# Where the key weights are loaded and the first tiles are normalised in a transformer block's forward and backward pass

## The chip, the cores and the metric

The kernel runs on one core of one Trainium2 chip. The metric is device time in microseconds, the median of several executions; lower is better. The engines are TensorE (PE; its weight loads are PEld), VectorE (DVE), ScalarE (ACT), GpSimd (POOL) and SyncE (SP), which only issues DMAs here. Each engine works through its own queue in program order.

## The reference

One block of a transformer with 2048 rows of width 640, and the gradients of all its inputs:

```python
h  = x + A_ref(layernorm(x), wqkv, wo)         # linear attention, 32 heads of 20
h2 = h + B_ref(layernorm(h), w1, w3, w2)       # silu(x @ w1) * (x @ w3) @ w2, F = 1728
# in A_ref:
q, k, v = split(x @ wqkv)
phi = lambda t: where(t > 0, t + 1, exp(t)) + 1e-6
pq, pk = phi(q), phi(k)
kv = einsum("bhsd,bhse->bhde", pk, v);  z = sum_s(pk)
o = (pq @ kv) / (pq . z + 1e-6);        return o @ wo
```

The outputs are h2 and the gradients of x, wqkv, wo, w1, w3 and w2 for a given `grad_out`, all bfloat16. `layernorm` takes the mean off a row and divides by the root of its variance plus 1e-5.

## The kernel before, in words

The 2048 rows are 16 tiles (ST) of 128 rows; the width of 640 is 5 chunks (DT) of 128, or two halves (HD) of 320. The order of all work is written out by hand: whatever is emitted first on an engine runs first there, and a DMA is issued in the order of the queue that issues it.

**The start (L115 to L195).** SP issues x tile 0, tile 1, the first column half of the key weights (`load_wq(2, 3)`), x tile 2, the second half (`load_wq(3, 4)`), x 3, x 4 and 5; then transposing loads of `w2T` and of the output's gradient (`g2T`), and the rest of x. ScalarE first runs one tiny Exp, which loads its table. TensorE runs 34 warm-up matmuls (L468).

**A tile's way through the first loop (L528 ff.).** For each tile t:
1. VectorE takes statistics (`stat`, L148 two `bn_stats`, L151 the aggregate, L154 variance plus epsilon), and POOL the power of -1/2 (L155, `ln_rs`).
2. `p1_norm` (L247) normalises x in place, on VectorE (L161), for tiles 10, 12 and 14 on ScalarE (L166, which needs a bias that POOL makes at L170). From tile 8 on it also issues a DMA transpose into `pqT` (L251).
3. Up to tile 7, `p1_tr` (L253) transposes the five chunks on TensorE into a PSUM tile `tr`, and ScalarE copies it to `pqT` (L260).
4. `p1_mm` (L274) multiplies the turned tile by the key weights, in two halves of five matmuls (L268), into a PSUM tile `big` of which there are two. The transposes of tile t+1 are emitted between the two halves (`between`).
5. `phi` (L290) has ScalarE read the sums twice, Exp (L295) into `mq` and Relu (L296) into `rq`, three buffers each; its two closing instructions on VectorE (L299, L300) are held back in a list `held` and emitted later.

Tile 0 is an exception (RAW = 1): its x is only centred, and the factor is given to ScalarE as the scale of its activations (L535); its keys use two PSUM tiles of their own, so that ScalarE can start on the first half. `p1_scale` (L262) multiplies x of tile 0 afterwards, on VectorE (L264).

The table `v_steps` says what VectorE does in step t of the loop, in this order: ("S", n) statistics of tile n, ("N", n) `p1_norm`, ("C", n) `p1_scale`, and R, which takes the oldest pair out of `held`. The letters A, B and L are `p1_norm` calls that come after `phi(t)`. Where t stands in `QT` = (6, 7, 9, 11), `q_tile` does the query product of tile 0, 1, 2, 3 in the same way as the keys, after the "A" step. In steps 3 to 6 `ghh_chunk` adds five matmuls of 512 columns (L395), which need `w2T` and `g2T`. From step 7 on `m_part` (L425) accumulates phi(k)ᵀ x over the tiles (needing the finished x of those tiles), and x is stored to DRAM (`xn_out`).

**After the loop** come more query tiles, the heads' denominators (`r_prod` on POOL, L367, `r_row` on VectorE, `r_T` DMA transposes), `load_w2T(4 * P, 8 * P)` (L624), and, when the last `m_part` is done, the reload of x tiles 0 to 5 (L641, for the residual). `f2_wT` (L701) then makes the product weights `Wp` and turns them by DMA transposes (L709); the first use of `Wp` is at L657.

**Later stages.** `q_parts` (L1205) makes the five blocks of QT, each turned by a DMA transpose on SP (L1226), while `load_xnT` (L1237) issues transposing loads on the same queue; the third of these stands before `part(20)` (L1315), which emits the rest of `q_parts`. The next product (L1388) reads all of QT. The last stage (L1556 ff.) makes the gradients of w1 and w3 in 35 jobs; the results of the first seven are stored in two pieces each.

Of the kernel before, what the change touches and what calls it, by code (L numbers as in the profile page):

```python
# [55 lines left out]
def kernel(  # L56
# [74 lines left out]
    class Stats:  # L131
# [13 lines left out]
        def part(self, src, t, j, mid=None):  # L145
            if j == 0:
                self.st[t] = cp.tile([P, 2, 6], F32, name="st6", bufs=4)
            V.bn_stats(out=self.st[t][:, j, :], in_=src[:, t, j * HD:(j + 1) * HD])  # L148
            if j == 0:
                return  # L150
            V.bn_aggr(out=self.mv[:, t, :], in_=self.st.pop(t)[:])  # L151
            if mid is not None:
                mid()
            V.tensor_scalar(out=self.ve[:, t:t + 1], in0=self.mv[:, t, 1:2], scalar1=EPS_LN, scalar2=None, op0=ALU.add)  # L154
            G.tensor_tensor(out=self.rs[:, t:t + 1], in0=self.ve[:, t:t + 1], in1=mhalf[:, 0:1], op=ALU.pow)  # L155
# [86 lines left out]
    RAW = 1  # L242
# [10 lines left out]
    def p1_tr(t, parts=((0, DT),)):  # L253
        xn = x_sb[:, t, :]
        for a, b in parts:
            tr = ps.tile([P, DT, P], BF16, name="tr", bufs=2)
            for c in range(a, b):
                T.transpose(tr[:, c, :], xn[:, c * P:(c + 1) * P], ident[:])

            A.copy(out=pqT[:, a:b, t * P:(t + 1) * P], in_=tr[:, a:b, :])  # L260
# [29 lines left out]
    def phi(acc, dst, t, parts=None):  # L290

        mq, rq = parts or phi_tiles()
        if parts is None:
            kw = dict(scale=ln1.rs[:, t:t + 1]) if t < RAW else {}
            A.activation(two(mq[:]), acc[:, :, 0:HD], AF.Exp, **kw)  # L295
            A.activation(two(rq[:]), acc[:, :, 0:HD], AF.Relu, **kw)  # L296

        def rest():
            V.tensor_scalar(out=mq[:], in0=mq[:], scalar1=1.0, scalar2=1e-6, op0=ALU.min, op1=ALU.add)  # L299
            V.tensor_tensor(out=dst, in0=mq[:], in1=rq[:], op=ALU.add)  # L300
        held.append(rest)
# [201 lines left out]
    def load_wo():  # L503
# [24 lines left out]
    for t in range(ST):  # L528
        first = None
        if t < RAW:  # L530
            first = phi_tiles()
            kh = [ps.tile([P, 512], F32, name="k0", tag="m", bufs=2) for _ in range(2)]

            def act(i, j):
                A.activation(first[i][:, j * HD:(j + 1) * HD], kh[j][:, 0:HD], (AF.Exp, AF.Relu)[i],  # L535
                             scale=ln1.rs[:, t:t + 1])

            def between():
                act(0, 0)
                p1_tr(t + 1)  # L540
                act(1, 0)
            k = p1_mm(t, D, between, kh)
            act(0, 1)
            act(1, 1)
        else:
# [78 lines left out]
    load_w2T(4 * P, 8 * P)  # L624
# [3 lines left out]
    m_part(4, range(5))  # L628
    q_tile(8)
# [11 lines left out]
    load_x(0, 6)  # L641
# [302 lines left out]
    def kv3():  # L944
# [5 lines left out]
        (f2_wT, 4), (phi_rest,), (q_late, 14), (r_T, 4), (r_head, 5), (r_prod, 7),  # L950
# [654 lines left out]
```

## Time and profile before

| what | us |
|---|---|
| median of 3 runs | 819.78 (819.46 to 819.9) |
| the profiled execution's own time | 820.36 |
| its span, first to last instruction | 818.6 |
| TensorE busy in the span | 811.6 |
| VectorE, ScalarE, GpSimd busy | 452.7, 324.8, 131.7 |
| first key matmul of tile 0 | 6.61 |
| key matmuls of tile 3 | 12.68 |

The tables below are read so: a timeline row has the start in us from the span's start, the duration in us, the engine, the line, the operation, what it writes <- reads, the shapes, the count, and in brackets the idle time before it and what ended that. A row with a count above 1 has several instructions merged, and its duration runs to the end of the last. Idle time of an engine that is not the bottleneck costs nothing.

### The profile page before, as it was taken

To read this page: it belongs to the slowest core of one execution; us is meant where nothing else is said; L and a number is where in the kernel's file an instruction comes from. 1 tells how busy PE (TensorE), PEld (TensorE's weight loads), DVE (VectorE), ACT (ScalarE), POOL (GpSimd) and SP (SyncE) were. 2 spreads that over 40 slices of the span, in tenths; PEclk is the share of its full clock that TensorE was granted. 3 is DMA by queue.
4 is the path that set the end of the run, shared out by engine and by line. 5 is a ranking of instruction groups with operands and counts; after the bars stand their busy time and mean duration, and the time that the engine had idled before them with its cause. 6 is when DMAs were issued, how large, how long until landed. Compare 5 with 4: busy or idle time off the path is not lost.

```text
span 818.6 us, 13711 instructions
## 1 busy us (share of the span) xinstructions
PE 811.6 (99%) x5261; PEld 501.6 (61%) x5292; DVE 452.7 (55%) x973; ACT 324.8 (40%) x609; POOL 131.7 (16%) x198
## 2 busy tenths in 40 slices
PE   9999999999999999999999999999999999999998
PEld 6777544555555555754577777777777777544444
DVE  7859997998898566300057777772781544200000
ACT  7856688665565666011112212222212334211111
POOL 2243333323222212100001111110220000000000
PEclk9999999999999999999999999999999999999999
DMA  9899899696485556999877877269994888979991
GB/s 262 207 242 277 206 276 302 207 244 174 128 209 158 169 168 168 239 254 243 233 178 181 218 194 193 58 111 181 269 217 93 179 193 153 249 175 235 221 239 37
DMA packets 335889, 162.46 MB, mean 198 GB/s; under 512 B 252560, under 2 KB 329072, under 8 KB 335824
## 3 DMA queue, kind: packets, MB, share of 16 engines
q1 hardware_dynamic: 291920, 120.68, 63.8%
q0 software_dynamic: 7328, 24.48, 8.9%
q10 hardware_dynamic: 36576, 16.42, 8.2%
q8 instruction: 41, 0.67, 0.3%
q14 instruction: 24, 0.20, 0.1%
HBM read 47.09 MB, written 53.43 MB: 123 GB/s over the span
## 4 chain that ended last, share of the span: by engine, by line
PE 96%; DMA 1%; ACT 1%; DVE 1%; issue 0%; SPq 0%; POOL 0%; DVEq 0%
PE mm L395 20%; PE job L1335 19%; PE ghn L1131 14%; PE gxn L1504 8%; PE gw L1086 7%; PE big L268 4%; PE o L913 4%; PE o L859 3%; PE gwo L1219 3%; PE macc L430 3%; PE gr L1188 3%; PE dkv L1441 3%; PE at L657 2%; DMA wqkv<-in_A_wqkv_dram 1%; PE dkv L1369 1%; DMA tri<-tri 1%
## 5 line engine op out<-in xcount | busy, mean ns | idle before, releaser
L1335 PE MATMUL job<-gb,hnN 128*128 128x496 bf16 (+3 forms) x576 | 116.8, 366 | 0.0
L1131 PEld LDWEIGHTS <-ggb 128*128 128x128 bf16 x864 | 84.5, 98 | 33.0
L395 PE MATMUL mm<-pqT,w 128*128 128x512 bf16 x396 | 93.2, 379 | 0.5
L1335 PEld LDWEIGHTS <-hnN 128*128 128x128 bf16 x576 | 55.8, 98 | 61.0
L395 PEld LDWEIGHTS <-w 128*128 128x128 bf16 x540 | 52.6, 98 | 62.9 <-issue 0.6
L1339 ACT CAST obs<-job 128x496 bf16<-128x496 f32 (+4 forms) x56 | 28.5, 510 | 123.6 <-PE job L1335 123.6
L1131 PE MATMUL ghn<-w13a,ggb 128*128 128x320 bf16 x448 | 63.5, 299 | 0.0
L1146 DVE SCALAR_TENSOR_TENSOR wb<-gs,hnb 128x640 f32<-128x640 bf16 x16 | 13.2, 825 | 88.1 <-ACT gs L1143 88.1
L1131 PE MATMUL ghn<-w13b,ggb 128*128 128x320 bf16 x416 | 61.4, 299 | 0.0
L395 PE MATMUL mm<-g2T,w2T 128*128 128x512 bf16 x228 | 58.8, 379 | 0.6
L1086 PE MATMUL gw<-hb,g 128*128 128x512 bf16 (+2 forms) x316 | 58.4, 345 | 0.2
L1086 PEld LDWEIGHTS <-g 128*128 128x128 bf16 x320 | 31.3, 98 | 27.0
L420 ACT CAST ghh<-mm 128x512 bf16<-128x512 f32 x48 | 28.2, 588 | 48.2 <-PE mm L395 41.4
L1196 POOL TENSOR_TENSOR sz<-Zb,g_h 128x640 f32<-128x640 bf16 x16 | 20.2, 1262 | 163.7 <-DVE g_h L1197 163.7
L796 ACT ACTIVATE sig<-mm 128x512 bf16<-128x512 f32 x56 | 33.7, 602 | 25.0 <-PE mm L395 21.6
L1143 ACT ACTIVATE gs<-ghn 128x640 bf16<-128x640 f32 x16 | 11.3, 705 | 76.0 <-PE ghn L1131 76.0
L395 PEld LDWEIGHTS <-w2T 128*128 128x128 bf16 x260 | 25.4, 98 | 23.4
L268 PEld LDWEIGHTS <-pqT 128*128 128x128 bf16 x320 | 30.7, 98 | 13.5 <-ACT pqT L260 0.9
L268 PE MATMUL big<-wqkv,pqT 128*128 128x320 bf16 x250 | 38.4, 299 | 0.2
L1335 PEld LDWEIGHTS <-g 128*128 128x128 bf16 x320 | 31.0, 98 | 11.5
L832 DVE TENSOR_TENSOR gate<-gate,sig 128x1024 bf16<-128x1024 bf16 x28 | 19.3, 689 | 33.9 <-ACT gate L807 31.1
L1091 ACT CAST gw2o<-gw 128x512 bf16<-128x512 f32 (+2 forms) x20 | 10.4, 519 | 66.6 <-PE gw L1086 25.3
(217 smaller groups left out, 1391.2 us busy)
## 6 DMA issues: line engine op xcount, KB each, us to landing
hh_d<-hhT SPq DMA_DIRECT2D x24, 256.0 KB, 2.8
gg_d<-gate POOLq DMA_DIRECT2D x24, 256.0 KB, 4.4
gg_d<-ghh POOLq DMA_DIRECT2D x24, 256.0 KB, 4.1
ggb<-gg_d SPq DMA_DIRECT2D x6, 896.0 KB, 5.3
ggb<-gg_d ACTq DMA_DIRECT2D x6, 832.0 KB, 5.7
ggb<-gg_d SPq DMA_DIRECT2D x2, 1728.0 KB, 13.9
pk_d<-pk_all SPq DMA_DIRECT2D x4, 640.0 KB, 5.4
g<-in_grad_out_dram SPq DMA_DIRECT2D x4, 640.0 KB, 5.7
```

Source lines behind the costliest of these rows:

```text
L268: T.matmul(acc, lhsT=pqT[:, c, t * P:(t + 1) * P], rhs=wqkv[:, c, n0:n0 + HD], start=(c == 0), stop=(c == DT - 1))
L395: T.matmul(acc[:], lhsT=w[:, c, fc * P:(fc + 1) * P], rhs=rhs[:, c, :], start=(c == 0), stop=(c == DT - 1))
L420: A.copy(out=ghh[n // 2][:, n % 2, :], in_=acc[:])
L430: T.matmul(macc[m][j][:, 0:n], lhsT=pk_all[:, t, m * P:(m + 1) * P], rhs=x_ext[:, t, j * HD:j * HD + n], start=(t == 0), stop=(t == ST - 1))
L796: A.activation(sig[:, i, :], gp[:], AF.Sigmoid)
L859: T.matmul(accs[i, j][:, 0:HD], lhsT=hhT[c][:, fc, i * P:(i + 1) * P], rhs=w2[:, fc, j * HD:(j + 1) * HD], start=(first and fc == 0), stop ...
L913: T.matmul(o2["ps"][:, 0:HD], lhsT=hhT[c][:, fc, i * P:(i + 1) * P], rhs=w2[:, fc, j * HD:(j + 1) * HD], start=(fc == 0), stop=(fc == FT - 1))
L1086: T.matmul(acc[:, 0:fw], lhsT=g2[:, t, m * P:(m + 1) * P], rhs=hb[b][:, t, 0:fw], start=(t == 0), stop=(t == ST - 1))
L1131: T.matmul(acc[:, j, 0:HD], lhsT=ggb[t // 2][:, k, lo:lo + P], rhs=rhs[:, j * HD:(j + 1) * HD], start=(k == 0), stop=(k == NG - 1))
L1335: T.matmul(acc[:, 0:n], lhsT=lhs[:, t, m * P:(m + 1) * P], rhs=rhs(t), start=(t == 0), stop=(t == ST - 1))
L1339: A.copy(out=ob, in_=acc[:, 0:n])
L1504: T.matmul(acc[:, j, 0:HD], lhsT=g, rhs=wqT[:, k, j * HD:(j + 1) * HD], start=(k == 0), stop=(k == 14))
```

## The change

- The key weights are loaded by ScalarE's queue in two pieces of rows (chunks 0 and 1, then chunks 2 to 4, all 640 columns), and x tiles 4 and 5 by that queue too; SP issues x tiles 1, 2 and 3 ahead of everything else.
- `first_mm` does tile 0's keys chunk by chunk, both halves in a `big` tile, with the transposes of tile 1 after the second chunk.
- RAW = 5: tiles 0 to 4 are only centred, and the factor goes to ScalarE's activations. `p1_scale` multiplies those tiles of x later, now on GpSimd.
- VectorE in place of ScalarE copies the turned tiles 2 and 3 out of PSUM; from t = 3 on, the transposes of tile t+1 come after both halves of tile t.
- `v_steps` is written anew for this, and four of eight further warm-up matmuls are left out.
- x tiles 0 to 3 are reloaded before the `w2T` load, which is moved behind `r_head(3)` and `m_part(4, range(5))` and split in two; tiles 4 and 5 are reloaded after `f2_wT(4)`.
- `load_xnT(2)` comes after `part(20)`; five instead of seven jobs store in two pieces.

```diff
-        def part(self, src, t, j, mid=None):
+        def part(self, src, t, j, mid=None, end=True):
...
-            if j == 0:
-                return
+            if j and end:
+                self.end(t, mid)
+
+        def end(self, t, mid=None):
             V.bn_aggr(out=self.mv[:, t, :], in_=self.st.pop(t)[:])
...
+    def load_wk(a, b):
+        A.dma_start(out=wqkv[:, a:b, D:2 * D], in_=wq_v[:, a:b, D:2 * D])
+
+    for t in (1, 2, 3):
+        load_x(t, t + 1)
     A.activation(sg[:], zero[:], AF.Exp)
-    load_wq(2, 3)
-    load_x(2, 3)
-    load_wq(3, 4)
-    load_x(3, 4)
-    load_x(4, 6)
+    load_wk(0, 2)
+    load_wk(2, DT)
+    load_x(4, 6, A.dma_start)
...
-    RAW = 1
+    RAW = 5
...
-            A.copy(out=pqT[:, a:b, t * P:(t + 1) * P], in_=tr[:, a:b, :])
+            copy(out=pqT[:, a:b, t * P:(t + 1) * P], in_=tr[:, a:b, :])
 
     def p1_scale(t):
         xn = x_sb[:, t, :]
-        V.tensor_scalar(out=xn, in0=xn, scalar1=ln1.rs[:, t:t + 1], scalar2=None, op0=ALU.mult)
+        G.tensor_scalar(out=xn, in0=xn, scalar1=ln1.rs[:, t:t + 1], scalar2=None, op0=ALU.mult)
...
+    def first_mm(between):
+        acc = p1_acc()
+        for c in range(DT):
+            for j in range(2):
+                T.matmul(acc[:, j, 0:HD], lhsT=pqT[:, c, 0:P], rhs=wqkv[:, c, D + j * HD:D + (j + 1) * HD],
+                         start=(c == 0), stop=(c == DT - 1))
+            if c == 1:
+                between()
+        return acc
...
-    warm_up(8, p1_acc()[:, 0])
-    stat(1)
-    p1_norm(1)
-    ln1.part(x_sb, 2, 0)
-    ln1.part(x_sb, 2, 1)
+    warm_up(4, p1_acc()[:, 0])
+    for t in (1, 2):
+        ln1.part(x_sb, t, 0)
+        ln1.part(x_sb, t, 1, lambda: center(t))
     ln1.part(x_sb, 3, 0)
-    p1_norm(2)
-    ln1.part(x_sb, 3, 1)
-    ln1.part(x_sb, 4, 0)
-    p1_norm(3)
-    ln1.part(x_sb, 4, 1)
+    ln1.part(x_sb, 3, 1, end=False)
...
-    v_steps = {1: (R, ("N", 4)), 2: (("S", 5), R, ("N", 5)), 3: (("S", 6), R, ("N", 6), ("C", 0)),
-               4: (("S", 7), R, ("N", 7), ("S", 8)), 5: (R, ("N", 8), ("S", 9)), 6: (R, ("N", 9), ("S", 10)),
-               7: (("S", 11), R, R, ("A", 10), ("L", 11)), 8: (("S", 12), R, R, ("S", 13)),
-               9: (("N", 13), R, ("S", 14), ("B", 12)), 10: (R, R, ("S", 15)), 11: (R, ("A", 14), ("L", 15))}
-    V_OPS = {"S": stat, "N": p1_norm, "C": p1_scale}
+    v_steps = {1: (("E", 3), ("P", 4, 0)), 2: (("P", 4, 1), ("E", 4), R), 3: (("S", 5), R, ("N", 5), ("C", 0)),
+               4: (("S", 6), R, ("N", 6), ("C", 1)), 5: (("S", 7), R, ("N", 7), ("S", 8), ("C", 2), ("C", 3)),
+               6: (R, ("N", 8), ("S", 9), ("C", 4)), 7: (R, R, ("N", 9), ("S", 10), ("S", 11), ("A", 10), ("L", 11)),
+               8: (("S", 12), R, R, ("S", 13)), 9: (("N", 13), R, ("S", 14), ("B", 12)), 10: (R, R, ("S", 15)),
+               11: (R, R, ("A", 14), ("L", 15))}
+    V_OPS = {"S": stat, "N": p1_norm, "C": p1_scale, "E": lambda t: ln1.end(t, lambda: center(t)),
+             "P": lambda t, j: ln1.part(x_sb, t, j, end=False)}
...
-            k = p1_mm(t, D, (lambda: p1_tr(t + 1)) if t + 1 < XT_DMA else None)
+        turn = (lambda: p1_tr(t + 1, copy=V.tensor_copy if t in (1, 2) else A.copy)) if t + 1 < XT_DMA else None
+        k = p1_mm(t, D, turn, int(t > 2)) if t else first_mm(turn)
...
-    load_w2T(4 * P, 8 * P)
     dmaG(out=m_v[:, 1:4, :], in_=mbs[:, 1:4, :])
     r_head(3)
     r_prod(5)
     m_part(4, range(5))
+    load_x(0, 4)
+    load_w2T(4 * P, 6 * P)
+    load_w2T(6 * P, 8 * P)
...
-    load_x(0, 6)
...
-        (f2_wT, 4), (phi_rest,), (q_late, 14), (r_T, 4), (r_head, 5), (r_prod, 7),
+        (f2_wT, 4), (load_x, 4, 6), (phi_rest,), (q_late, 14), (r_T, 4), (r_head, 5), (r_prod, 7),
...
+    part(20)
     load_xnT(2)
-    part(20)
...
-                halves = ((a, c), (c, b)) if i * DT + m < 7 else ((a, b),)
+                halves = ((a, c), (c, b)) if i * DT + m < 5 else ((a, b),)
```

More of the change, by code (lines that the diff above doesn't have):

```diff
@@ L184, in load_wq, with load_x @@
         dma(out=wqkv[:, :, a * HD:b * HD], in_=wq_v[:, :, a * HD:b * HD])
-    def load_x(a, b):
-        dma(out=x_sb[:, a:b, :], in_=xS[:, a:b, :])
-    load_x(1, 2)
-    A.activation(sg[:], zero[:], AF.Exp)
-    load_wq(2, 3)
-    load_x(2, 3)
-    load_wq(3, 4)
-    load_x(3, 4)
-    load_x(4, 6)
+    def load_x(a, b, q=dma):
+        q(out=x_sb[:, a:b, :], in_=xS[:, a:b, :])
+    def load_wk(a, b):
+        A.dma_start(out=wqkv[:, a:b, D:2 * D], in_=wq_v[:, a:b, D:2 * D])
+    for t in (1, 2, 3):
+        load_x(t, t + 1)
+    A.activation(sg[:], zero[:], AF.Exp)
+    load_wk(0, 2)
+    load_wk(2, DT)
+    load_x(4, 6, A.dma_start)
     mask = cp.tile([P, DT, M_MAX], BF16, name="mask")
@@ L251, in p1_norm, with p1_tr @@
             dmaT(out=pqT[:, :, t * P:(t + 1) * P], in_=xn)
-    def p1_tr(t, parts=((0, DT),)):
+    def p1_tr(t, parts=((0, DT),), copy=A.copy):
         xn = x_sb[:, t, :]
@@ L272, in p1_acc, with p1_mm @@
         return ps.tile([P, 2, 512], F32, name="big", bufs=2)
-    def p1_mm(t, n0, between=None, halves=None):
-        acc = p1_acc() if halves is None else None
+    def p1_mm(t, n0, between=None, at=0):
+        acc = p1_acc()
         for j in range(2):
-            p1_half(acc[:, j, 0:HD] if halves is None else halves[j][:, 0:HD], t, n0 + j * HD)
-            if j == 0 and between is not None:
+            p1_half(acc[:, j, 0:HD], t, n0 + j * HD)
+            if j == at and between is not None:
+                between()
+        return acc
+    def first_mm(between):
+        acc = p1_acc()
+        for c in range(DT):
[3 more added lines that the diff above has]
+            if c == 1:
                 between()
@@ L288, in phi_tiles, with phi @@
         return [p1.tile([P, D], BF16, name=n, bufs=3) for n in ("mq", "rq")]
[L290 to L296, printed above, removed]
+    def phi(acc, dst, t):
+        mq, rq = phi_tiles()
+        kw = dict(scale=ln1.rs[:, t:t + 1]) if t < RAW else {}
+        A.activation(two(mq[:]), acc[:, :, 0:HD], AF.Exp, **kw)
+        A.activation(two(rq[:]), acc[:, :, 0:HD], AF.Relu, **kw)
         def rest():
@@ L528 @@
     for t in range(ST):
[L529 to L545, printed above, removed]
-            k = p1_mm(t, D, (lambda: p1_tr(t + 1)) if t + 1 < XT_DMA else None)
+        turn = (lambda: p1_tr(t + 1, copy=V.tensor_copy if t in (1, 2) else A.copy)) if t + 1 < XT_DMA else None
+        k = p1_mm(t, D, turn, int(t > 2)) if t else first_mm(turn)
         steps = v_steps.get(t, (R,) * len(held))
@@ L551 @@
             elif step[0] in V_OPS:
-                V_OPS[step[0]](step[1])
-        phi(k, pk_all[:, t, :], t, first)
+                V_OPS[step[0]](*step[1:])
+        phi(k, pk_all[:, t, :], t)
         for when in ("A", "B", "L"):
```

## The prediction

> **What bounds the kernel now.** I read the page's busy shares, then the chain that ended last, then the engines' busy time by stage, then the timeline of the first 40 us.
>
> ```profile
> PE 811.6 (99%) x5261; PEld 501.6 (61%) x5292; DVE 452.7 (55%) x973; ACT 324.8 (40%) x609; POOL 131.7 (16%) x198
> ...
> PE 96%; DMA 1%; ACT 1%; DVE 1%; issue 0%; SPq 0%; POOL 0%; DVEq 0%
> ```
>
> TensorE carries the chain and hardly ever waits: the most a better order can give is the few microseconds in which it does. But over the whole span VectorE at 55% hides a stage. Busy time by stage (us of PE, PEld, DVE, ACT, POOL):
>
> ```profile
> 6.20:14.00 7.80, 6.99 (x61) 4.46 (x59) 6.59 (x20) 6.38 (x12) 2.04 (x4) 1.00 1.12 256
> 14.00:25.00 11.00, 10.89 (x78) 7.00 (x78) 10.14 (x34) 10.16 (x17) 2.58 (x5) 1.00 0.96 311
> ```
>
> From 14 to 25 us VectorE works 10.1 of 11 us: in the tile loop it is nearly as full as TensorE. The timeline shows TensorE's waits at the start, and behind them ScalarE waiting for VectorE:
>
> ```profile
> 6.61 0.84 PE L268 MATMUL k<-wqkv,pqT 128*128 128x320 bf16 x5 [0.18 <-DMA wqkv<-in_A_wqkv_dram]
> ...
> 8.14 0.84 PE L268 MATMUL k<-wqkv,pqT 128*128 128x320 bf16 x5 [0.41 <-DMA wqkv<-in_A_wqkv_dram]
> ...
> 10.73 0.52 PEld L268 LDWEIGHTS <-pqT 128*128 128x128 bf16 x5 [0.44 <-ACT pqT L260]
> ...
> 12.68 0.52 PEld L268 LDWEIGHTS <-pqT 128*128 128x128 bf16 x5 [0.44 <-ACT pqT L260]
> ...
> 29.15 0.70 ACT L295 ACTIVATE mq<-big 128x640 bf16<-128x640 f32 x1 [0.20 <-DVE pk_all L300]
> ...
> 32.40 0.70 ACT L295 ACTIVATE mq<-big 128x640 bf16<-128x640 f32 x1 [0.76 <-DVE pk_all L300]
> ```
>
> Two waits are for key weights, two for ScalarE's copy of a turned tile. Two more follow later, 0.4 us at 85.6 (Wp's transposes) and 0.5 us at 566.5:
>
> ```profile
> 558.77 3.34 SPq L1242 DMA_TRANSPOSE xnT<-xn_d  x1
> ...
> 562.21 1.22 SPq L1226 DMA_TRANSPOSE tri<-tri  x1
> ...
> 566.50 0.78 PE L1388 MATMUL gkvT<-tri,woT 128*128 128x140 bf16 x10 [0.47 <-DMA tri<-tri]
> ```
>
> **Start.** Tile 0's own chain stays; its second ScalarE copy starts near 5.6, and other rows give 0.74 from such a copy's start to the next matmul (9.99 to 10.73): first matmul at 6.25, not 6.61. The weights: before, two column halves landed at 6.6 and 8.1 (issue 1.73 + 4.8, 2.77 + 5.3). Now ScalarE issues them after its first activation ends (2.30), three DMAs of about 0.5 each (SP rows 0.43 to 0.52), done by 3.8, before its first work at 4.50 (0.7 of cover; what exceeds it would delay tile 0). The first piece is only 320 KB. 560 KB (x tile 2 and the second half) took the 1.5 us between the halves, so x 2, x 3 and piece 1 (640 KB) need about 1.8 us from 3.1: 5 to 5.5. Piece 2 (480 KB), beside w2T's transposes, which SP now issues from about 2.7 and not 4.3: 6.3 to 8.1; I take 6.9, and 7.1 is when it is needed. Then, at 0.136 us a matmul and 0.056 a transpose: tile 1 starts at 8.0 (was 8.82). VectorE's copies of tiles 2 and 3 out of PSUM are not in the trace; L1422's copies take 0.28 at 256 columns and 0.35 at 384, so 0.49 at 640, at most ScalarE's 0.69; I take 0.49. The copy starts 0.49 after the transposes: tile 2 at 9.7 (10.73), tile 3 at 11.4 (12.68). **Gain 1.3.** The four warm matmuls left out (4 x 0.107) ran in waiting time. From tile 3 on the transposes come after both halves: ScalarE's copy then hides under ghh_chunk (5 matmuls, 1.08).
>
> **VectorE's account decides whether that gain lives.** From start-to-start times in the rows: a statistic S 1.23 (0.91 stats pair, 0.245, 0.075), a rest R 0.83 (0.42 + 0.41), a norm N 0.36, a centring 0.30. After the first copy (9.60): E3, half of 4, the wait for and copy of tile 3 (to 11.3), half of 4, E4, R: 13.2. Step 3 (S R N, 2.42) 15.6; step 4 18.05; step 5 (two S) 21.7; step 6 24.1; step 7 (R R N S S, 4.48) 28.6. N11 now has no R ahead of it to hide POOL's power (0.77 wait, as before at 35.06: 0.67), 29.7; S12 30.95; then at last the R of q_tile(0), 31.8. Before, that R ended at 29.9 (29.40 + 0.49). mq and rq are three deep, so phi(8) waits for it: 31.9 instead of 30.34, ends at 33.3; only then is the second "big" bank free for q_tile(2), which before started at 32.10 (30.74 + 1.36). The same happens once more, since q_tile(1)'s R now stands behind N13's wait: q_tile(3) at 39.5, before 37.81. **The gain is used up and 1.7 us lost**, with no cost yet for the scaling moved to GpSimd. Scaled activations (0.79 for 0.70) and the first wait behind N5 (0.26) are inside these sums.
>
> **The five scalings on GpSimd.** This operation isn't in the trace on POOL. Its neighbours: a product of 320 columns takes 0.79, one of 640 columns with two inputs 1.26; half of that is 0.63. I take 1.0, bounds 0.63 and 1.26. POOL itself has room. But see the one mq row that met such products:
>
> ```profile
> 59.05 0.97 DVE L381 TENSOR_TENSOR hx<-hx,rden 128x640 bf16<-128x640 bf16 x1
> 59.94 1.86 DVE L299 TENSOR_SCALAR mq<-mq 128x640 bf16<-128x640 bf16 x1
> ...
> 60.07 1.54 POOL L367 TENSOR_TENSOR pr<-hx,Zb 128x320 f32<-128x320 bf16 x2
> ```
>
> Elsewhere that instruction takes 0.32. Here it ends at 61.80, 0.33 after 61.47, which is 0.14 before POOL's second product ends: it stood until POOL was through. The statistics (L148) keep their 0.48 beside POOL. Now C0, C1, C2 and C4 become ready 0.84 us after a statistic's L154, in the middle of the R behind it, and take the next turn: N5, N6, N8 and an R wait 1.0 - 0.14 = 0.86 each, while C3 runs beside S9. 4 x 0.86 = 3.4, all on the path above. Loop: 1.7 + 3.4 = 5.1 later (bounds 0.49 and 1.12 a block: 3.7 to 6.2).
>
> The Trainium skill (SBUF — State Buffer, section "Who interferes with whom") says that of a VectorE instruction in a two-port mode and a GpSimd instruction, whichever issues first holds the shared pair for the whole instruction and the other is blocked; the row at 59.94 agrees (1.86 for 0.32). By that rule the sum would be anywhere from 0 to 3.4 for this part, by who is first; the sum above does not use it.
>
> **The rest.** The x reload in two parts and w2T in two: Wp's transposes no longer queue behind 960 KB, so the 0.4 at 85.6 goes (bounds 0 and 0.4). w2T's first half is issued near 75 and lands within 5.4 to 6.2 (its rows), before its use at 82.7; if late it would cost the difference. r_T(4) waits for one more issue on SP, 0.5, used 7 us later. load_xnT(2) behind the last QT transpose: ScalarE's copy ended at 561.45, SP was busy to 562.11; the transpose goes 0.7 earlier and 0.5 of waiting goes. xnT(2) is read some 30 us later. Two output stores undivided in the last stage: TensorE is continuous there, 0. Together -0.9.
>
> **Sum.** +5.1 - 0.9 = +4.2 on the profiled execution (820.36, of which the span is 818.6 and 1.8 lie around it): 824.6. The median of the runs shown is 819.78, 0.6 lower, so 824.0. What a measurement of this kernel can tell from no change is about 0.2%, 1.6 us.
>
> **Rivals.**
> *GpSimd costs nothing* (VectorE wins every turn and the scalings fall under the statistics, which don't wait): +1.7 - 0.9 = +0.8, 820.6; with a late piece 2 (+0.6) 821.2. For it: 1.23 of statistics could hold 1.0 of scaling. Against: the mq row waited through two products.
> *Faster*: the buffers behind phi(8) decide. If q_tile(0)'s R ends before 30.3, TensorE keeps the start's 1.3 and the 0.9: 817.6. For it: all of TensorE's waits are addressed. Against: it needs VectorE 1.5 us earlier than its rows add up to, and before the change ScalarE waits there already (0.20, 0.76).
> *The clock*: matmuls ran at 0.107 us a 128-column matmul until 6.19 and at 0.056 after. With a thinner start the step could come later; 3.4 us later would make 1.7 us more, 825.7. The Trainium skill (TensorE: Matmul & The Clock Gate, Part 1) has a free-running window of about 3.4 us of activity; the single step at 6.19 here can't show its phase.
>
> **How the numbers follow.** Forecast 0.62 (its own range 822.5 to 826.0: the GpSimd bounds, piece 2 to 0.7 late, the copies' upper end 0.4); GpSimd free 0.22; faster 0.10; clock 0.06. Slower by over 0.2% (above 821.4): 0.62 + 0.06 + 0.04 of the second case; the same 0.18; faster 0.10. The range takes in the forecast and the second case from 820.0 to 826.0, and leaves out the faster case and part of the others.
>
> **What would show it.** Right: tile 3's key matmuls near 11.4; N5 or N6 at well over 0.44, or starting late beside a POOL scaling; q_tile(2) and q_tile(3) waiting for a PSUM bank after ScalarE waited for VectorE; no wait at 566. Wrong: N5, N6 and N8 at 0.44 beside POOL; TensorE continuous from 14 to 48 us; or the first matmul late for its weights.

## The result, and the profile after

The changed kernel takes 829.65 us (median of 6 runs, 826.95 to 830.88) against 819.84 for the kernel before on the same chip (6 runs, 819.21 to 821.52): ratio 1.0115, 95% interval 1.0104 to 1.0126, so 9.4 us slower (8.5 to 10.3). The forecast was 4.2 us. The profiled execution of the changed kernel has a span of 828.3 us, 9.7 more than before. Below, a ratio r is given as (r - 1) x 820 us. Waits of TensorE in the text count from start to start; the bracket of a row is some 0.16 us less, because a matmul's modelled duration (0.30) reaches past the start of the next one (0.136 later).

Busy shares and the chain that ended last, of the changed kernel:

```profile
PE 813.2 (98%) x5257; PEld 500.7 (60%) x5288; DVE 455.9 (55%) x974; ACT 324.2 (39%) x605; POOL 140.7 (17%) x203
...
PE 90%; DMA 4%; DVE 3%; SPq 2%; ACT 1%; issue 0%; POOL 0%; DVEq 0%; ACTq 0%
```

TensorE's share of the chain fell from 96% to 90%: the time is in TensorE's waits, not in its work. Transfers now hold 4% of the chain and VectorE 3%. Busy time by stage (stretch, its length, then PE, PEld, DVE, ACT, POOL, granted clock, DMA share, GB/s):

```profile
6.20:14.00 7.80, 5.76 (x49) 3.70 (x47) 5.25 (x18) 4.88 (x7) 1.65 (x3) 1.00 1.23 189
14.00:25.00 11.00, 10.03 (x77) 6.61 (x77) 10.25 (x30) 8.35 (x14) 6.33 (x7) 1.00 1.06 326
25.00:36.36 11.36, 8.55 (x60) 5.71 (x60) 10.03 (x27) 6.79 (x11) 8.69 (x10) 1.00 0.58 131
36.36:39.78 3.42, 2.90 (x13) 1.51 (x11) 2.58 (x9) 2.49 (x4) 0.97 (x2) 0.50 0.78 240
```

Until 14 us TensorE has only 5.8 us of work in 7.8, and the transfers are slower (189 GB/s, before 256). From 25 to 36 it loses another 2.8 us, while GpSimd, at 2.6 us in the second stretch before, is the second busiest engine. And behind that, for 3.4 us, TensorE's granted clock is 0.50. These are TensorE's waits in the loop, and two of those behind it:

```profile
8.23 0.98 PE L290 MATMUL big<-wqkv,pqT 128*128 128x320 bf16 x6 [1.07 <-DMA wqkv<-in_A_wqkv_dram]
...
13.40 1.53 PE L272 MATMUL big<-wqkv,pqT 128*128 128x320 bf16 x10 [0.73 <-DVE pqT L264]
...
16.13 1.24 PE L408 MATMUL gp<-g2T,w2T 128*128 128x512 bf16 x4 [0.92 <-DMA g2T<-in_grad_out_dram]
...
35.41 1.94 PE L272 MATMUL big<-wqkv,pqT 128*128 128x320 bf16 x10 [2.76 <-ACT rq L309]
...
37.86 2.31 PE L272 MATMUL big<-wqkv,pqT 128*128 128x320 bf16 x9 [0.52 <-ACT rq L309]
...
98.80 0.85 PE L652 MATMUL at<-Wp,pqT 128*128 128x320 bf16 x5 [1.36 <-DMA Wp<-pkx]
...
595.27 1.52 PE L1436 MATMUL dkv<-small,xnT 128*128 128x320 bf16 x10 [0.82 <-DVE gp L1439]
```

The second key-weight piece, the copy of tile 3, g2T; then tile 9's keys, which wait 2.9 us (2.76 in the row) for a PSUM bank; then Wp's fifth block, and at 595 VectorE's g_k, the gradient of the keys, which itself waits 2.2 us for pkb (phi of the keys, loaded back from DRAM). The QT wait at 566 is gone.

To locate the time, I subtract the start times of the same TensorE instruction in two profiles. Against before, the changed kernel is 1.7 us late at the first m_part matmul (29.43), 6.7 late at the m_part matmul ahead of tile 12's keys (45.85), 9.3 at 105 us, 8.7 at 576 (QT's wait gone) and 9.7 at the end. So three places: the start 1.7, the rest of the loop 5.0, behind the loop 3.0. This is one execution: a second profile of the changed kernel (after_again, below) has 0.7, 4.6 and 5.4, and a second one of the kernel before (before_again) is itself 0.8 late at the end of the loop and 1.8 at the end.

Rows of GpSimd, VectorE, ScalarE and TensorE's weight loads ahead of the long wait:

```profile
17.17 1.95 POOL L268 TENSOR_SCALAR x_sb<-x_sb,ln_rs 128x640 bf16<-128x640 bf16 x1
17.28 0.92 DVE L163 TENSOR_SCALAR x_sb<-x_sb,ln_mv,ln_rs 128x640 bf16<-128x640 bf16 x1
...
25.37 3.82 POOL L268 TENSOR_SCALAR x_sb<-x_sb,ln_rs 128x640 bf16<-128x640 bf16 x2
...
29.16 0.62 POOL L157 TENSOR_TENSOR ln_rs<-ln_ve,mhalf 128x1 f32<-128x1 f32 x1
...
29.47 0.49 DVE L313 TENSOR_TENSOR pk_all<-mq,rq 128x640 bf16<-128x640 bf16 x1
...
29.88 0.92 DVE L163 TENSOR_SCALAR x_sb<-x_sb,ln_mv,ln_rs 128x640 bf16<-128x640 bf16 x1
...
32.11 0.57 POOL L157 TENSOR_TENSOR ln_rs<-ln_ve,mhalf 128x1 f32<-128x1 f32 x1 [0.39 <-DVE ln_ve L156]
...
33.07 0.92 ACT L168 ACTIVATE x_sb<-x_sb,nb,ln_rs 128x640 bf16<-128x640 bf16 x1 [2.81 <-POOL nb L172]
...
34.26 0.10 PEld L272 LDWEIGHTS <-pqT 128*128 128x128 bf16 x1 [1.95 <-DMA pqT<-x_sb]
```

One scaling takes 1.95 us, twice the estimate. The norm beside it takes 0.92 instead of 0.44, so VectorE loses 0.48 to it, and gets its turn long before the scaling ends at 19.12. C2 and C3 hold GpSimd's queue for 3.8 us, and rs9 (the power for tile 9), ready to start near 27.6, comes at 29.16. Here that costs nothing: VectorE is busy with two rests until tile 9's norm, which follows at 29.88 without a wait. Tile 10's power does not stand behind a scaling either; GpSimd waits 0.39 us for VectorE's variance. What is late is VectorE. ScalarE then stands 2.8 us before the norm of tile 10, which needs the bias nb10, with q_tile(1)'s activations, which free tile 9's bank, behind it. But the last row shows a second late product: tile 9's turned columns let the weight load go only at 34.26. A third is q_tile(0)'s rest, for which ScalarE's next activation waits until 36.5. One wait is named, and three things were late side by side.

### The profile page after: what moved, and what is told of

It is laid out like the page before. It is cut to its first block, busy times and chain, and to the rows that moved or that the text cites. A ratio compares the mean times of both kernels' runs of the same rounds, so it can differ in the third digit from the quotient of the medians.

```text
span 828.3 us, 13713 instructions
## 1 busy us (share of the span) xinstructions
PE 813.2 (98%) x5257; PEld 500.7 (60%) x5288; DVE 455.9 (55%) x974; ACT 324.2 (39%) x605; POOL 140.7 (17%) x203
## 4 chain that ended last, share of the span: by engine, by line
PE 90%; DMA 4%; DVE 3%; SPq 2%; ACT 1%; issue 0%; POOL 0%; DVEq 0%; ACTq 0%
PE mm L408 20%; PE job L1330 18%; PE ghn L1126 14%; PE gxn L1499 8%; PE gw L1081 7%; PE o L908 4%; PE o L854 3%; PE gwo L1214 3%; PE gr L1183 3%; PE big L272 2%; PE dkv L1436 2%; PE macc L443 2%; PE at L652 2%; DMA g2T<-in_grad_out_dram 1%; DMA pkb<-pk_d 1%; SPq L1237 1%
## 5 line engine op out<-in xcount | busy, mean ns | idle before, releaser
L1141 DVE SCALAR_TENSOR_TENSOR wb<-gs,hnb 128x640 f32<-128x640 bf16 x16 | 13.2, 825 | 88.1 <-ACT gs L1138 88.1
## 6 DMA issues: line engine op xcount, KB each, us to landing
ggb<-gg_d SPq DMA_DIRECT2D x2, 1728.0 KB, 13.2
```

## The experiments

Each edit is against the kernel named; times are compared with the kernel before on the same chip. "Late by" is again the start of the same TensorE instruction against the first profile of before.

### Parts of the change undone

**v_scale**: the scalings on VectorE.

```
-        G.tensor_scalar(out=xn, in0=xn, scalar1=ln1.rs[:, t:t + 1], ...)
+        V.tensor_scalar(out=xn, in0=xn, scalar1=ln1.rs[:, t:t + 1], ...)
```

> The changed kernel with the five scalings of tiles 0 to 4 on VectorE instead of GpSimd. Theory (the scalings cost through GpSimd's queue: 1.95 us each, C2 and C3 together 3.8 us ahead of rs9, and from there N9, S10, nb10, ScalarE's norm of tile 10, q_tile(1), and the PSUM bank of tile 9's keys): rs9 comes right behind its statistic, TensorE's wait of 2.9 us before tile 9's keys shrinks to under 1.3 us, the clock stays whole behind it, and 1.6 + 1.7 us go: 826.3 us. Rival (VectorE's own account is what runs out, as the prediction has it, 1.7 us lost without any scaling): five times 0.3 us on VectorE more than make up for what GpSimd blocked, the wait stays above 2.3 us and the clock still drops: 829 to 830 us.

827.39 us, ratio 1.0090 (1.0077 to 1.0103): 2.0 us less than the change (3.4 less than after_again), between the two. In the profile the wait before tile 9's keys is still 2.2 us and the clock still halves; this execution, 829.17, is the slowest of the five, and the other four have a mean granted clock of 1.000. VectorE now runs from 10 to 36 us with hardly a gap. Tile 9's transposing DMA, which follows its norm, is issued at 25.80 before, at 28.86 here and at 30.83 in the change. The 3.06 us here are VectorE's own: four scalings more at some 0.34 from start to start, two copies at 0.41, and one rest (0.83) that the change's order puts ahead of that norm, 3.0 in all. That the DMA is 2.0 later still in the change is not all GpSimd's: x tile 4 landed at 12.44 there and at 10.80 here. In after_again, where it landed at 11.35, the DMA is issued at 29.74, 0.9 behind v_scale. VectorE's rows account for those 3.94 us against before: two copies (0.82), the rest (0.83), four norms 0.48 longer and two `mq` 0.40 and 0.26 longer beside scalings (2.58 together), less tile 0's scaling (0.30), 3.93.

**sp_order**: the row pieces and x tiles 4 and 5 on SyncE, in the order of before.

```
-        A.dma_start(out=wqkv[:, a:b, D:2 * D], in_=wq_v[:, a:b, D:2 * D])
+        dma(out=wqkv[:, a:b, D:2 * D], in_=wq_v[:, a:b, D:2 * D])
...
-    for t in (1, 2, 3):
-        load_x(t, t + 1)
+    load_x(1, 2)
     A.activation(sg[:], zero[:], AF.Exp)
     load_wk(0, 2)
+    load_x(2, 3)
     load_wk(2, DT)
-    load_x(4, 6, A.dma_start)
+    load_x(3, 4)
+    load_x(4, 6)
```

> The changed kernel with the two row pieces of the key weights and x tiles 4 and 5 back on SyncE's queue, in the order of the kernel before (x 1, piece, x 2, piece, x 3, x 4 and 5, and only then the transposing loads of w2T and g2T). Theory (the transposing loads, issued earlier beside ScalarE's loads, make x 4 and g2T late): x 4 and 5 land near 9.4 and g2T near 12.8 us, the waits before tile 3 (0.9) and before the first ghh chunk (1.1) go, tile 4's keys start near 15.5 instead of 17.2, and all but little of the 1.7 us comes through, since VectorE's chain hangs on tile 4's statistics: 828.0 us. Rival (GpSimd's and VectorE's chain behind tile 5 sets tile 9 whatever the loads do): the wait before tile 9's keys grows by what was saved, 829.6 us.

830.93 us, ratio 1.0132 (1.0115 to 1.0148). The loads came as expected (x 4 and 5 at 9.27, g2T at 12.79), the waits for tile 3 and g2T went, and nothing was gained: in this execution x 6 to 9 landed at 18.1 (before 15.6, with the same issue time), tiles 5 and 6 waited 0.8 and 1.2 us for VectorE, and tile 9's keys again 2.9. By the time the rival had it. That VectorE's chain alone sets tile 9 is not shown by this profile, since the late x 6 to 9 delayed that chain too.

**late_undone**: all edits behind the loop undone.

```
+    load_w2T(4 * P, 8 * P)
     dmaG(out=m_v[:, 1:4, :], in_=mbs[:, 1:4, :])
...
-    load_x(0, 4)
-    load_w2T(4 * P, 6 * P)
-    load_w2T(6 * P, 8 * P)
...
     ps.release()
+    load_x(0, 6)
...
-        (f2_wT, 4), (load_x, 4, 6), (phi_rest,), ...
+        (f2_wT, 4), (phi_rest,), ...
...
-    part(20)
     load_xnT(2)
+    part(20)
...
-                halves = ((a, c), (c, b)) if i * DT + m < 5 else ((a, b),)
+                halves = ((a, c), (c, b)) if i * DT + m < 7 else ((a, b),)
```

> The changed kernel with its edits behind the tile loop undone: x reloaded in one piece after the loop, w2T in one transposing load ahead of the m store, xnT(2) before the last QT transposes, seven divided stores. Theory (these edits cost time: 1.0 us at 83 for mT behind the x reload, 1.5 us at 98.8 for Wp's fifth block, 0.35 us net near 566 to 595): 2.9 us less, 826.8 us, with a Wp wait of 0.4 and a QT wait of 0.5 back. Rival (the prediction's: they gain 0.9 us): 830.5 us.

826.42 us, ratio 1.0076 (1.0063 to 1.0089): 3.2 us less than the change, as the theory had it, and the waits for Wp and g_k are gone. But the waits of 0.4 for Wp and 0.5 for QT, which should have come back with the old order, did not, and the wait for mT (the turned m) at 81, which I had put down to these edits, is 2.4 us here. It isn't theirs.

**norm10_late**: ScalarE's norm of tile 10 behind q_tile(1).

```
-                7: (R, R, ("N", 9), ("S", 10), ("S", 11), ("A", 10), ("L", 11))
+                7: (R, R, ("N", 9), ("S", 10), ("S", 11), ("B", 10), ("L", 11))
```

> The changed kernel with ScalarE's norm of tile 10 put behind q_tile(1)'s two activations in ScalarE's queue, so that q_tile(1)'s PSUM bank no longer waits for nb10. Theory A (this order is the cause of the 2.9 us wait): tile 9's keys start near 32.5 instead of 35.4 and 2.5 us or more go, 827.0 us. Theory B (VectorE as a whole is 3 to 5 us late, and three of its products are late side by side: nb10, tile 9's turned columns at 34.2, and q_tile(0)'s rest, which frees the exp's buffer of tile 8): tile 9's keys start near 34.4, q_tile(2) not sooner than now (37.9), and the loop gains under 0.5 us: 829.3 us.

831.43 us, ratio 1.0138 (1.0124 to 1.0152). TensorE and ScalarE of this kernel:

```profile
33.09 1.53 PE L272 MATMUL big<-wqkv,pqT 128*128 128x320 bf16 x10 [0.65 <-DMA pqT<-x_sb]
...
36.31 0.70 ACT L308 ACTIVATE mq<-big 128x640 bf16<-128x640 f32 x1 [2.52 <-DVE hx L313]
...
37.66 1.94 PE L272 MATMUL big<-wqkv,pqT 128*128 128x320 bf16 x10 [3.03 <-ACT rq L309]
```

Tile 9's keys start 2.3 us earlier, then at once bounded by tile 9's columns. q_tile(2) starts at 37.66 (37.86 in the change): the whole wait has moved to it, behind q_tile(0)'s rest. Theory A falls, theory B holds.

**v_scale_acopy**: v_scale with `copy=A.copy` for tiles 2 and 3 too.

> The changed kernel with the scalings on VectorE and also the copies of turned tiles 2 and 3 back on ScalarE: VectorE does 0.9 us less than in v_scale. Theory B (VectorE's account sets the loop): N9 0.8 to 0.9 us earlier, and after 0.2 to 0.5 us of waits for ScalarE's copies at the start the loop ends about 0.5 us earlier: 826.9 us. Rival (VectorE's account is not the bound; the start's copies are): 0.5 to 0.8 us slower than v_scale, 828.0 us.

828.78 us, ratio 1.0106 (1.0090 to 1.0121): not faster than v_scale, the rival's value. At the first m_part matmul it is 1.3 us late (v_scale 0.2), with waits of 0.7 and 0.3 us for ScalarE's copies and 0.8 for a late g2T; from there to tile 12 it loses 3.3 us where v_scale loses 4.6. So the loop may have got VectorE's 0.8 us back and the start used it up; but the second weight piece also landed later here (8.15, in v_scale 7.21), and one profile of each can't part the two.

### Parts of the change alone, and doubled costs, in the kernel before

**v_more**: VectorE work added.

```
+    def more(n):
+        for _ in range(n):
+            V.tensor_scalar(out=pk_all[:, ST - 1, :], in0=x_sb[:, 0, :], scalar1=0.5, ...)
...
     3: (..., ("C", 0), ("X", 3)), 4: (..., ("N", 7), ("X", 3), ("S", 8)), 5: (R, ("N", 8), ("X", 3), ("S", 9))
```

> The kernel before with nine more VectorE instructions of 128 x 640 (0.34 us from start to start each, 3.1 us in all), whose result nobody uses, three each in steps 3, 4 and 5 of the tile loop. Theory B (VectorE has no slack in the loop: q_tile(0)'s rest is 0.4 us ahead of its use, tile 9's turned columns 1.5 us): tile 9's keys 1.6 us later, q_tile(2) 2.3 to 2.7 us later, 822.6 us. Rival (VectorE has 3 us of slack there, and what slows the changed kernel is GpSimd or the loads): under 0.5 us, 820.3 us.

823.68 us, ratio 1.0050 (1.0036 to 1.0064): 4.1 us. The loop ends 2.93 us late for 3.1 us of added work: VectorE has no slack there at all, and tile 9's DMA is issued at 28.79, 2.99 late. This carries VectorE's part of the explanation.

**gps_more**: the same `more`, once each, as a GpSimd scaling by rs, in steps 3, 4, 5 (two) and 6. **gps_spread**: one each in steps 3, 4, 5, 7 and 10.

```
-            V.tensor_scalar(out=pk_all[:, ST - 1, :], in0=x_sb[:, 0, :], scalar1=0.5, ...)
+            G.tensor_scalar(out=pk_all[:, ST - 1, :], in0=x_sb[:, 0, :], scalar1=ln1.rs[:, 0:1], ...)
```

> The kernel before with five more GpSimd instructions of 128 x 640 with a scale read per row, as the change has them, in steps 3, 4, 5, 5 and 6 of the tile loop; nobody uses their result. Theory (1.95 us each; VectorE's norms beside them take 0.92 instead of 0.44 and its mq up to 0.4 more, 2 to 2.6 us in all on a VectorE without slack, and rs9 or rs10 stands behind them in GpSimd's queue): 2.0 to 3.0 us more, 822.3 us. The prediction's step (an instruction of 1.0 us that blocks VectorE for 0.86 four times, 3.4 us): 823.2 us. Rival (no cost, VectorE wins every turn): under 0.4 us, 820.2 us.

> As gps_more (the kernel before with five more GpSimd scalings that nobody uses), but spread out: one each in steps 3, 4, 5, 7 and 10, and none between two statistics that follow closely, so that a power stands behind one scaling at most. Theory (GpSimd's queue: in gps_more rs9 and rs11 came 1.8 and 2.2 us late behind scalings, and tile 10's norm and N11 with them): the loop ends 1 to 2 us late instead of 4.45, 821.5 to 822.0 us. Rival (the shared port: each scaling costs VectorE its time wherever it stands): 5 x 0.5 to 0.9 us, 824 us or more, as gps_more.

gps_more: 826.30 us, ratio 1.0067 (1.0049 to 1.0085), 5.5 us; the loop ends 4.45 late. gps_spread: 823.36 us, ratio 1.0035 (1.0021 to 1.0049), 2.9 us; the loop ends 2.13 late. The rows of gps_more:

```profile
26.50 3.94 POOL L515 TENSOR_SCALAR pk_all<-x_sb,ln_rs 128x640 bf16<-128x640 bf16 x2
30.40 0.63 POOL L155 TENSOR_TENSOR ln_rs<-ln_ve,mhalf 128x1 f32<-128x1 f32 x1
...
31.61 0.92 ACT L166 ACTIVATE x_sb<-x_sb,nb,ln_rs 128x640 bf16<-128x640 bf16 x1 [3.07 <-POOL nb L170]
...
34.31 0.45 DVE L161 TENSOR_SCALAR x_sb<-x_sb,ln_mv,ln_rs 128x640 bf16<-128x640 bf16 x1 [2.24 <-POOL ln_rs L155]
```

A power that takes 0.6 us stands behind 3.9 us of scaling, ScalarE waits 3.1 us for what follows from it, and VectorE, which has no slack, stands idle for 2.2 us behind the next scaling. With five scalings apart from each other, two of them in later steps, about half of the cost is gone. That points to GpSimd's queue for this half. The exact share isn't shown: in six other executions with the loop unchanged (before_again, before_late, before_xw, before_xnT2, x_split, xnT_tail) it ended between 0.05 early and 1.3 us late. The rest goes with what VectorE loses beside each scaling (norms of 0.92 for 0.44, again seen) and a power that one scaling still delays by 0.6.

**start_only**: only the start's transfers as in the change, tile 0's keys in their order, and four warm matmuls less.

```
-    load_x(1, 2)
-    A.activation(sg[:], zero[:], AF.Exp)
-    load_wq(2, 3)
...
+    for t in (1, 2, 3):
+        load_x(t, t + 1)
+    A.activation(sg[:], zero[:], AF.Exp)
+    load_wk(0, 2)
+    load_wk(2, DT)
+    load_x(4, 6, A.dma_start)
```

> The kernel before with only the start's transfers changed: key weights in two row pieces and x tiles 4 and 5 from ScalarE's queue, tile 0's keys in the order of the row pieces, four warm matmuls less; tiles 1 to 4 are normalized as before. Theory C (the first key matmul comes 0.8 us sooner, but the transposing loads now start among the first loads: x 4 lands 3 us later, g2T 2.4 to 3.3, x 6 to 9 2 us): tile 4's keys later and about 1 to 1.7 us lost: 821.2 us. Rival (the prediction's start: 1.3 us gained, of which VectorE lets little through): 819.0 to 819.8 us.

822.37 us, ratio 1.0019 (1.0010 to 1.0027): 1.6 us lost. Theory C's size, but not quite its place. The first key matmul comes at 5.87 (before 6.61). Then VectorE has x 1 late (at 4.94, before 3.60, since ScalarE's piece is issued ahead of it), and tile 2's transposes wait 0.7 us for its norm; the loop ends 0.8 late. That is no more than the unchanged loop shows in before_again (0.8) and before_late (1.3), and the other 1.1 us of this profile are in waits for mT and Wp, which the edit does not touch. The runs show that 1.6 us are lost, not where.

**before_late**, **before_xw**, **before_xnT2**: the edits behind the loop in the kernel before, all, only the x reload and w2T, only xnT(2).

> The kernel before with only the change's edits behind the tile loop (x reloaded in two parts, w2T in two, both ahead of q_tile(8); xnT(2) behind the last QT transposes; five divided stores). Theory (mT's lateness at 83 us is not theirs, since it stood there with them undone; theirs are Wp's fifth block and pkb, which land late in some runs): Wp's and QT's waits of 0.4 and 0.5 go, up to 1.5 + 1.0 us come: between 819.2 and 822.0 us. The prediction's own value: 0.9 us less, 819.1 us. Rival (they cost 2.9 us, as the difference between two profiles first looked): 822.9 us.

> The kernel before with only the x reload in two parts and w2T in two, both ahead of q_tile(8). Theory (two more transposing loads stand on SyncE's queue right ahead of Wp's five, each holding the queue for 1.3 us or more, and the fifth then lands beside the pq store and the second x part): Wp's waits become 1.6 us instead of 0.4, 1.2 us more: 821.0 us. The prediction's value: 0.4 us less, 819.4 us. Rival (most of the 3.4 us of all the late edits are here): 822.5 us or more.

> The kernel before with only xnT(2) put behind the last QT transposes. Theory (QT's 0.5 us goes, but xnT(2), xnT(3) and wqT(0) then stand one behind the other and push the pkb loads 2.4 us later, so that g_k comes late for dkv): a new wait of 1.0 to 1.6 us near 580 to 595, 0.4 to 1.0 us more: 820.5 us. The prediction's value: 0.5 us less, 819.3 us.

before_late 824.00 us, ratio 1.0042 (1.0028 to 1.0055), 3.4 us; before_xw 822.11 us, 1.0021 (1.0011 to 1.0032), 1.7 us; before_xnT2 823.03 us, 1.0019 (1.0006 to 1.0031), 1.6 us. The two parts add up to the whole, and the whole to what late_undone took away, each within about 1 us. The times carry this, not the profiles: in before_late's, 1.3 of 3.5 us lie in the loop, which is unchanged. **x_split** keeps w2T in one piece where it was:

```
     m_part(4, range(5))
+    load_x(0, 4)
     q_tile(8)
...
-    load_x(0, 6)
...
+        (f2_wT, 4), (load_x, 4, 6), (phi_rest,), ...
```

> The kernel before with x reloaded in two parts as in the change (tiles 0 to 3 ahead of q_tile(8), 4 and 5 behind f2_wT(4)), but w2T left whole in its old place. Theory (w2T's two transposing issues ahead of Wp are what holds SyncE's queue): Wp's five are issued 1.3 us apart without a hole, no loss, 0 to 0.4 us gained: 819.6 us on a kernel before of 819.8. Rival (the second x part and the pq store beside Wp's fifth block): 1 us or more lost, 821.0 us.

820.89 us, ratio 1.0009 (0.9999 to 1.0018): no loss that can be told from none. SyncE's queue of before_xw, then of x_split:

```profile
75.30 0.53 SPq L187 DMA_DIRECT2D x_sb<-in_A_x_dram  x1
75.89 5.00 SPq L457 DMA_TRANSPOSE w2T<-in_B_w_dram  x2
81.06 8.15 SPq L710 DMA_TRANSPOSE Wp<-pkx  x5
```

```profile
72.55 3.00 SPq L457 DMA_TRANSPOSE w2T<-in_B_w_dram  x1
75.65 1.22 SPq L385 DMA_TRANSPOSE pqT<-hx  x1
76.96 0.53 SPq L187 DMA_DIRECT2D x_sb<-in_A_x_dram  x1
79.64 6.50 SPq L709 DMA_TRANSPOSE Wp<-pkx  x5
```

Two halves of w2T hold SyncE for 5.0 us where the whole took 3.0, and right ahead of Wp: Wp's first issue is 1.4 us later and its five take 8.15 instead of 6.50. In x_split's profile Wp's wait is gone, and 0.6 us are lost just behind it, at 98. This points to w2T, divided and moved behind the x reload, and not to the divided reload. It isn't shown: the intervals of before_xw and x_split overlap, no run parts the dividing from the moving, and other profiles go both ways. With w2T whole Wp's five took up to 7.4 us and TensorE waited up to 1.8 (start_only); with the halves, in fill9 and fill9_again, they took 6.5 and it did not wait.

SyncE's queue of before_xnT2, where pkb was issued from 572.66 before:

```profile
564.76 7.11 SPq L1242 DMA_TRANSPOSE xnT<-xn_d  x2
571.92 3.98 SPq L1299 DMA_TRANSPOSE wqT<-in_A_wqkv_dram  x1
...
577.26 3.51 SPq L1410 DMA_DIRECT2D pkb<-pk_d  x4
```

Two xnT transposes and wqT now stand in one row ahead of pkb. g_k waits 2.5 us for pkb and TensorE 1.3 for g_k. All the profiles bear this out: of ten with `load_xnT(2)` in its new place and xnT(3) not moved, eight have such a wait at this point (0.5 to 1.6 us; fill9 and fill9_again have none), and of nine with the old order none. QT's wait of 0.6 is gone too, but that is not the edit's doing: of the nine profiles with the old order only the first one of before has it. **xnT_tail** moves xnT(3) behind the four pkb loads as well:

> The kernel before with xnT(2) put behind the last QT transposes, as in the change, and xnT(3) moved behind the four pkb loads, so that SyncE's queue comes to them when it did before. Theory (the change's loss here is that pkb is issued 2.4 us late): QT's wait of 0.5 to 0.6 us goes and no new one comes: 819.2 us on a kernel before of 819.8. Rival (xnT(3) now holds up the turned gm blocks behind it, or pkb's lateness is not the queue's): 820.5 us.

820.22 us, ratio 1.0009 (0.9993 to 1.0025). pkb is issued at 572.05 and the wait for g_k near 587 is gone, QT's too; but waits of 1.8 us (until 609.87) and 0.9 (until 628.02) take their place. SyncE now comes to the pkT transposes behind xnT(3) at 599.46, before at 591.25; that this is what makes those two late is likely and not shown. Neither theory's number; no gain either way. No version beat the kernel before.

### Scatter, and the clock

**before_again**, **after_again**: the two kernels once more.

> The kernel before itself, once more. If the waits for mT and Wp are fixed by the program, TensorE waits 0.4 us for Wp, as in the first profile, and not for mT; if they hang on when transfers happen to land, as before_xnT2 (1.2 and 0.9 us for Wp, with the same code up to 570 us) suggests, 0.4 to 2 us in all: 819.8 to 821 us.

> The changed kernel once more. Theory (the loop's 5 to 6.7 us are the program's, while the waits for mT and Wp scatter between executions): 828 to 830.5 us, tile 9's keys again 2.7 to 3 us late for their bank, a late wait of 1 us or more near 595.

before_again: 819.82 us (819.27 to 822.19), ratio 0.9996 (0.9983 to 1.0010). Its profile has a span 1.8 us longer than the first one, with waits of 1.3 us for mT and 0.7 for Wp: the same program, other landings. The loop ends 0.8 late, and QT's product runs without a wait:

```profile
567.39 1.73 PE L1388 MATMUL gkvT<-tri,woT 128*128 128x140 bf16 x25
```

after_again: 831.14 us, ratio 1.0132 (1.0116 to 1.0149), with 2.9 us before tile 9's keys, 1.0 for mT, 1.9 for Wp, 1.3 for g_k. The mT wait belongs to neither kernel in particular, and Wp's and mT's differ by a microsecond or two between executions (mT's from 0 to 2.4); only timed runs can price an edit there.

**fill9**, and **fill9_again** beside after_again: fillers where TensorE waits.

```
     for t in range(ST):
+        if t == 9:
+            warm_up(42, ps.tile([P, 512], F32, name="fill", tag="tr", bufs=2))
```

> The changed kernel with 42 small matmuls of ones (2.35 us at the full clock) in a PSUM bank of their own ahead of tile 9's keys, where TensorE waits 2.9 us. They compute nothing that is used. Theory (the wait itself halves the clock from 36.4 to 39.8, which costs 1.7 us on top of the wait): the clock stays whole, tile 9's keys start at 35.4 as in the changed kernel, tile 10's at 39.3 instead of 40.95: 828.0 us. Rival (the halving comes from something else, and the fillers only take the wait's place): 829.6 us; if they run into the keys, up to 830.5.

> The changed kernel with the 42 fillers ahead of tile 9's keys once more, beside after_again. If the halved clock has a price of its own: 1.5 to 2.3 us faster than after_again. If a wait for ScalarE takes its place (VectorE and ScalarE come no sooner): within 0.8 us of after_again.

fill9: 826.63 us, ratio 1.0087 (1.0071 to 1.0103); fill9_again: 830.22 us, ratio 1.0137 (1.0108 to 1.0167), beside 1.0132 of after_again. In both profiles the granted clock stays at 1.00 to the end; in after_again it is 0.5 from 34.52 to 37.94. Yet from the first m_part matmul to tile 12's keys the loss is 4.55 us in after_again and 4.49 and 4.46 in the two with fillers: instead of slow matmuls there are waits of 0.6, 1.1 and 0.5 us. By these three profiles the halved clock cost nothing in the loop. The times do not settle it: by their ratios, fill9 is 2.3 us better than the change when measured apart from it, and fill9_again 0.4 us worse than after_again side by side (by the medians 0.9 better), with two of its six executions at a mean clock of 0.996.

The mean granted clock is known for each execution; 0.998 over the span is what one halved stretch of 3.4 us comes to. In most kernels that have both kinds the halved ones are the slower: in v_scale 829.2 against 826.0 to 827.9, in late_undone 826.4 to 827.8 against 824.7 and 825.9, in after_again 831.1 to 832.6 against 829.2; in fill9 not (827.5 against 825.5 to 829.8). But a longer wait takes time and can halve the clock too, so this gives the clock no price either.

## Why the prediction was wrong

The direction, and that VectorE's account decides, were right. 824.0 was 5.6 us short of 829.65. By its own steps:

- **"The rest ... together -0.9."** This step failed most: its sign was wrong. Measured: +3.4 alone (before_late), 3.2 in the change (late_undone), so 4.1 to 4.3 of the 5.6 us. I followed each moved transfer to its reader ("lands before its use at 82.7", "read some 30 us later") and Wp and QT to what stood ahead of them, but not the moved transfers to those queued behind them. xnT(2), xnT(3) and wqT(0) in a row push pkb from 572.66 to 577.26 in before_xnT2, 2.6 us more than the 2.0 by which that execution was late there, and TensorE waits for what needs it. For w2T's halves, which hold SyncE for 5.0 us right ahead of Wp's issues in before_xw, the same is likely and not shown as well. The two waits that I credited, 0.4 for Wp and 0.5 for QT, were not fixed by the order at all: with the old order back in late_undone neither returned, and the kernel before itself has no QT wait in its second profile, and 0.7 for Wp.
- **"Start. Gain 1.3."** Failed: 1.6 us lost (start_only). ScalarE issued the pieces at 1.14 and 1.63, not after 2.30. That put them ahead of x 1 (5.07 in the change, before 3.60). The second piece, taken at 6.9 from a range up to 8.1, landed at 8.19 in the change, and between 7.05 (after_again) and 8.65 (norm10_late) in the nine profiles with this start; TensorE waited 1.2 us for it in the change and not at all in after_again. SyncE's transposing loads, now earlier beside ScalarE's, took 9.9 and 11.3 us to land instead of 6.2 and 5.4, and x 4 came at 12.44 instead of 9.38 (10.5 to 12.4 in the nine). Tile 3's keys started at 13.40, not 11.4 (12.31 in after_again).
- **"VectorE's account ... 1.7 us lost."** Right, and by more than the total shows. From the statistics of tile 5 to the end of q_tile(0)'s rest it has 13.2 to 31.8, 18.6 us. Measured: 21.2 in the change (15.23 to 36.41) and in after_again (14.14 to 35.33), which is the 18.6 and the 2.6 by which scalings lengthened VectorE's instructions. What was wrong is where it begins: 2.0 and 0.9 us later than 13.2, for want of the start's gain. v_more has the exchange rate: 3.1 us of work, 2.93 us of time. The prediction named q_tile(0)'s rest; two more products, tile 9's columns and nb10, were as late.
- **"The five scalings on GpSimd ... 3.4."** The mechanism held, both sizes were wrong, and the errors partly cancel. An instruction takes 1.95 us, outside the bounds of 0.63 and 1.26: the rows that I took for neighbours, products without a scale per row, were no bound. And VectorE lost 0.48 a norm, not 0.86, in four norms, and 0.66 in two `mq`: 2.6 us. By the times the scalings cost 2.0 (v_scale; 3.4 against after_again) more than on VectorE, and 5.5 alone in before (gps_more). There GpSimd's queue also held powers behind scalings, a cost that the sum did not have and that the change did not pay.
- **Luck.** The sum for the loop, 5.1 (3.7 to 6.2), lies near the 6.7 and 5.3 by which the loop ended late in the two profiles. In part this is chance: a start that lost instead of gaining was made up for by scalings that cost less than 3.4.
- **Rivals.** "GpSimd costs nothing" is out. "The clock" came at another place than I thought, at 36.4, as the effect of a wait, and with no price that the profiles show.

New sum: VectorE 3.0 to 4.1 (v_scale's count, v_more's time), GpSimd 2.0, start 1.6, behind the loop 3.2: 9.8 to 10.9, measured 9.4 (8.5 to 10.3) and, once more, 10.8 (9.5 to 12.2). The parts come from separate kernels, each known to about 1 us, and need not add up; that they do proves little.

On who holds the port: in the changed kernel four VectorE norms issued just behind a scaling's start took 0.92 for 0.44, and all ended while the scaling was still running. The Trainium skill (SBUF — State Buffer, section "Who interferes with whom") has the engine that issues first hold the pair of ports that VectorE and GpSimd share for its whole instruction; by that the norm at 17.28 would have ended after 19.12, and it ended at 18.20. Here the measurement decides. The row at 59.94, which the prediction counts for the rule, has the length of a block (1.86 for 0.32), but not the order: VectorE's instruction, which stood, starts 0.13 us ahead of GpSimd's product.

## What to carry to other kernels

When a transfer is moved, list what its queue issues next and when that is needed; the transfers behind it can pay, not its own reader (pkb, 1.3 us). A wait of half a microsecond in one profile may be absent from the next of the same kernel, as QT's was: look at a second one before its removal enters a sum. Work moved to an idle engine joins that engine's queue: if short instructions there feed the critical chain, a long one ahead of them can cost its whole length (2.2 us in gps_more). Where the profile names one wait at the end of a crowded stage, ask what would be late next: removing the named cause (norm10_late) only moved 2.3 us of wait to the next tile.

## What was not expected of the hardware

- A GpSimd scaling of 128 x 640 in bf16 with a scale per row took 1.88 to 1.97 us in most places, 2.2 to 2.3 in three, more than a two-input product of the same size (1.26).
- The same transposing load of w2T held SyncE's queue for anything from 3.0 us (x_split) to 4.6 (late_undone) when given whole, and its two halves, issued behind an x reload, for 3.9 (fill9_again) to 6.1 (v_scale).
- DMAs on ScalarE's queue were issued at 1.14 and 1.63 us in the changed kernel, though they come behind the first activation in the program: its table load ran from 0.81 to 2.09, itself until 2.30.
- The clock's steps lie on a grid: in the changed kernel it rose at 5.64 and halved from 36.36 to 39.78, in after_again from 3.80 and from 34.52 to 37.94. Both times 30.72 us lie between rise and fall, nine times the 3.41 that it stayed halved. The wait behind which it fell was 2.9 us. The Trainium skill (TensorE: Matmul & The Clock Gate, Part 1) gives a free-running window of 3.4 us, with which the grid agrees, and asks for a window of idleness; here a window that was about 2.5 us idle (32.95 to 36.36, the wait ending at 35.41) was enough. In v_scale 2.0 idle us in one such window were.
- One and the same kernel differed by 1.8 us between two profiles: loads issued in the first 14 us landed up to 1.1 us later, the loop ended 0.8 later, mT's wait was 1.3 and QT's was gone.
